# Two PSUM banks for the second part's products, and the scores' transposes in the scores' bank

## The chip, the cores and the metric

The kernel runs on one core of a Trainium2 chip. The metric is the device time of one execution in microseconds. A core has a matrix engine (PE, with its weight loads shown apart as PEld), a vector engine (DVE), an activation engine (ACT), a general engine (POOL), and a queue (SP) that here only issues transfers. PE writes its products into PSUM, which DVE and ACT read; the kernel uses PSUM as eight banks of 128 partitions by 512 fp32 columns.

## The reference

`x` and `v` have the shape (4, 11456, 128). A filter made by a small network from position embeddings is convolved with `x*v` along the sequence, the result is multiplied by `x`, and every token then goes through a top-1 mixture of 8 experts:

```python
h_filt = (np.maximum(pos_emb @ w1, 0.0) @ w2) * np.exp(-0.01 * pos)[:, None]
y = irfft(rfft(x * v, 2 * S) * rfft(h_filt, 2 * S))[:, :S]      # along the sequence
x = (x * y).reshape(B * S, D)
...
do_compute = x @ w_skip > 0
xc = x[do_compute]
logits = xc @ w_gate
e_idx = np.argmax(logits, axis=1)
gate_w = softmax(logits)[np.arange(len(xc)), e_idx]
for e in range(E):
    mask = e_idx == e
    y[mask] = gate_w[mask, None] * (np.maximum(xc[mask] @ w1[e], 0.0) @ w2[e])
out[do_compute] = xc + y
```

## The kernel before

The convolution is done as a discrete Fourier transform written as matmuls. `first_phase` and `freq_phase` do the forward transform, the product with the filter and most of the way back; they leave an intermediate array `zd` in DRAM. `out_phase`, the second part, does the last step of the transform, the multiplication by `x`, the choice of expert for every token, and the lists of tokens by expert. The experts' matmuls start inside it (`early_slots`) and go on after it (`late_slots`).

The second part goes over 32 chunks (`ch`) of 3 blocks (`blk`). All its instructions are put in order by hand: each function of a chunk or block has a lag in steps and a rank inside a step, and every engine runs its instructions in that order. In a step, by rank:

- `produced` (rank 0): `product` makes y by two matmuls (line 1031, PE; the profile shows four, as each fp32 one is done in two passes) from `zt`, loaded from `zd`, and DVE multiplies y by `x` into `xm` (line 1032). After it one piece of the experts' work is issued: matmuls into `mh` (lines 706 to 708) with their activation on ACT (`h`, line 732), copies of an expert's weights (`ws`, line 678, and `wd`, line 771), transposes of gathered tokens (line 695) with their copy (`hl`, line 697), or the second matmuls into `bank[2]` (line 789).
- `exp` (rank 1, ACT, line 1084).
- `score2` (rank 2): PE transposes the copied scores `lt` into `lgp` (line 1058) and ACT copies them to `lg` (line 1061).
- `choose` (rank 3, DVE).
- `turn` (rank 4): four transposes of the block before into `tp` (line 1044), copied by ACT to `xT` (line 1046).
- `total`, `measure`, `lay` (rank 4.4, lines 1105, 1121, 1136), `count` and `ranks` (rank 4.5, lines 1097, 1143 and 1144), `collect` (line 1176): small matmuls of the lists, once for a chunk.
- `score` (rank 4.9): four column groups of scores into `lp` (line 1052; eight in the profile), copied by ACT to `lt` (line 1054).
- `counted` (rank 6): ACT copies the counts `mine` (line 1101).

`route` reads the ranks `rk` on DVE (line 1150) ahead of `produced` in its step. The waits between engines are put in from what each instruction reads and writes; the code has no semaphores of its own.

PSUM of the second part before: one bank for `y`, one for `tp`, four called `bank` (0: the scores `lp` and the counts `mine`; 1: the small matrices of the lists; 2: the experts' second products; 3: the transposed scores `lgp`), two for `mh`.

Of the kernel before, what the change touches and what calls it, by code (L numbers as in the profile page):

```python
# [10 lines left out]
F32 = mybir.dt.float32  # L11
# [6 lines left out]
PSUM = bass.MemoryType.PSUM  # L18

B, S, D = 4, 11456, 128  # L20
E, F = 8, 1024
# [4 lines left out]
NS = NB * B  # L26
# [928 lines left out]
def out_phase(tc, i, out, zd, ex, consts):  # L955
# [6 lines left out]
    with (  # L962
        tc.tile_pool(name="slot", bufs=2, reuse_waits="tile") as eb,
    ):
      with (
        tc.manual_schedule(),
        tc.tile_pool(name="ob", bufs=2, reuse_waits="tile") as ob,
        tc.tile_pool(name="oz", bufs=2, reuse_waits="tile") as oz,
        tc.tile_pool(name="opy", bufs=1, space=PSUM, reuse_waits="tile") as opy,
        tc.tile_pool(name="opt", bufs=1, space=PSUM, reuse_waits="tile") as opt,  # L970
        tc.tile_pool(name="opl", bufs=1, space=PSUM, reuse_waits="tile") as opl,
        tc.tile_pool(name="eps", bufs=2, space=PSUM, reuse_waits="tile") as eps,
      ):
        wg, val, grid, cols, odd, rev, tri, ones = consts
        ex.space(eb)
        bank = [opl.tile([128, 512], F32, name=f"bank{k}") for k in range(4)]

        lp, lgp, mine = bank[0][:, 0:128], bank[3][:, 0:128], bank[0][0:E * NS, 128:129]
        rk, places = bank[1][:, 0:E * NS], bank[1][0:PQ, 96:96 + PL]
        sizes = bank[1][0:E, 128:134].rearrange("p (a b) -> p a b", a=3)  # L980
        lies, whole = bank[1][0:PQ, 134:135], bank[1][0:E * NS, 135:136]
# [309 lines left out]
def program(tc, i, out):  # L1291
# [5 lines left out]
    with tc.tile_pool(name="mc", bufs=1) as mc:  # L1297
        wf = mc.tile([128, 2 * E * F], F32, name="wf")
        fi = First(nc, i, x1d, x1f, mc, wf)
        spare = wf[:, fi.used:]  # L1300
        c3 = mc.tile([128, 2, 128], F32, name="c3")
        first_phase(tc, fi)
        nc.scalar.dma_start(c3, i["c3"])
        nc.scalar.dma_start(zd.rearrange("p h r w -> (p h) r w")[:, H2 * 2 * K1:], i["none"])
        later = {}

        def prepare():

            later["ex"] = Experts(tc, i, out, lists, mc, wf)
            yield  # L1310
            later["consts"] = out_consts(nc, i, mc)
            for e in range(E):
                if e % 2 == 0:
                    yield
                later["ex"].weights(e, 0)

            for e in range(E):
                if e != 1:
                    yield
                later["ex"].weights(e, 1)  # L1320
        freq_phase(tc, nc, i, fi, zd, c3, spare, prepare())
        out_phase(tc, i, out, zd, later["ex"], later["consts"])
# [55 lines left out]
```

## Time and profile before

| | |
|---|---|
| median of 3 runs | 1622.03 us (1619.08 to 1622.11) |
| profiled execution | 1621.31 us, span 1619.5 us |
| busy: PE / DVE / POOL / ACT | 95% / 74% / 68% / 49% of the span |
| second part begins / its last y starts | 735 us / 1165 us |

The span is from the first to the last instruction; the rest of the execution's time lies around it. In the views, a row of the order of time has the start in us, the duration, engine, line, operation, what is written <- what is read, the shape, and how many; in square brackets stand the idle time of the engine ahead of it and what ended it. A row of waits has who waited, for whom, the total in us, how many times, and the longest.

### The profile page before, as it was taken

The numbers are of one execution on the slowest core, as the hardware profiler recorded it, in microseconds if no ns is written. First come the engines' busy times: TensorE is split into PE (matmuls) and PEld (weight loads), VectorE is DVE, ScalarE is ACT, GpSimd is POOL, SyncE is SP. The second block draws the span as 40 slices with busy tenths as digits, with TensorE's granted clock in tenths as the row PEclk, the third lists the DMA queues.
The fourth block names the chain that finished last, engine by engine and source line by source line (L and its number), as shares of the span: only waits on it lengthen the run. The fifth ranks groups of instructions, "written<-read, shape, count | busy, mean of one in ns | idle before, by whom it ended". The sixth has DMA issues, their size and how long they took to land.

```text
span 1619.5 us, 26517 instructions
## 1 busy us (share of the span) xinstructions
PE 1537.8 (95%) x8272; PEld 960.9 (59%) x8272; DVE 1197.2 (74%) x2403; ACT 794.3 (49%) x1691; POOL 1094.7 (68%) x857
## 2 busy tenths in 40 slices
PE   7985999999999999998789999999989999999997
PEld 2552444444444444443356776666777888888997
DVE  1323877888788889995868777777767777777986
ACT  3552455444544544442345444444435555556774
POOL 1112988888888878870265729846587888777885
PEclk9996999999999999998989999999999999999999
DMA  7998999999999789968967878777521111111110
GB/s 269 334 349 317 377 377 374 357 333 331 327 343 328 262 265 313 315 209 297 312 209 241 254 230 256 245 245 238 176 67 37 46 46 46 45 37 39 37 36 21
DMA packets 200644, 361.92 MB, mean 223 GB/s; under 512 B 64842, under 2 KB 141018, under 8 KB 200462
## 3 DMA queue, kind: packets, MB, share of 16 engines
q1 hardware_dynamic: 181078, 316.98, 57.7%
q0 software_dynamic: 16704, 38.89, 8.5%
q10 hardware_dynamic: 2720, 4.34, 0.9%
q8 instruction: 67, 1.10, 0.3%
q14 instruction: 75, 0.61, 0.1%
HBM read 216.96 MB, written 145.69 MB: 224 GB/s over the span
## 4 chain that ended last, share of the span: by engine, by line
PE 81%; DVE 6%; DMA 6%; issue 4%; ACT 1%; POOL 1%; SPq 1%; ACTq 0%; DVEq 0%; POOLq 0%
PE ps L405 19%; PE xp L374 12%; PE bank L789 6%; PE ps L203 5%; PE y L1031 4%; PE my L841 4%; PE my L839 4%; PE my L840 4%; PE hp L706 4%; PE hp L708 4%; PE hp L707 4%; PE tp L1044 2%; PE mh L706 2%; PE bank L1052 1%; DMA ox<-xo 1%
## 5 line engine op out<-in xcount | busy, mean ns | idle before, releaser
L405 PE MATMUL ps<-y,c 128*128 128x512 f32 x720 | 331.3, 597 | 0.3
L472 POOL TENSOR_TENSOR y<-y,p 128x2048 f32<-128x2048 f32 x59 | 267.9, 4541 | 68.7 <-DVE p L394 68.7
L712 POOL DMA_INDIRECT out<-o,ids x186 | 202.9, 1091 | 136.9 <-DVE o L719 97.5
L405 PEld LDWEIGHTS ps<-y,c 128*128 128x128 f32 x720 | 133.4, 190 | 173.0 <-issue 155.1
L643 POOL DMA_INDIRECT xt<-out,ids x186 | 195.7, 1052 | 50.4 <-issue 32.1
L394 DVE TENSOR_TENSOR p<-xp,g 128x1024 f32<-128x1024 f32 x240 | 217.4, 947 | 0.0
L394 DVE TENSOR_TENSOR y<-xp,g 128x1536 f32<-128x1536 f32 x120 | 210.8, 1757 | 4.1
L828 DVE SCALAR_TENSOR_TENSOR hh<-hp,hh 128x1024 fp32r<-128x1024 f32 x130 | 158.4, 1218 | 66.7 <-ACT hh L827 66.7
L406 ACT COPY z<-ps 128x512 f32<-128x512 f32 x180 | 105.6, 586 | 178.2 <-PE ps L405 164.2
L827 ACT ACTIVATE hh<-hp 128x1024 fp32r<-128x1024 f32 x130 | 134.2, 1033 | 69.0 <-PE hp L708 69.0
L473 POOL TENSOR_TENSOR y<-y,p 128x1024 f32<-128x1024 f32 x59 | 139.0, 2357 | 4.6
L683 DVE TENSOR_TENSOR ws<-wf,ws 128x1024 fp32r<-128x1024 f32 x104 | 126.7, 1218 | 13.8 <-ACT ws L678 12.4
L616 POOL MEMSET idle<- 128x512 f16 x248 | 134.5, 542 | 0.3
L706 PE MATMUL hp<-hl,ws 128*128 128x512 f32 (+1 forms) x344 | 123.6, 359 | 2.2 <-DVE hh L828 1.4
L203 PE MATMUL ps<-wf,c 60*120 60x384 f32 x512 | 111.0, 530 | 13.7 <-DVE wf L186 13.6
L1031 PE MATMUL y<-zt,c 128*64 128x512 f32 x384 | 111.7, 648 | 12.7 <-DVE xm L1032 7.0
L374 PE MATMUL xp<-x,wf 128*128 128x480 f32 x256 | 117.8, 585 | 5.8 <-DMA x<-x1f 3.3
L789 PEld LDWEIGHTS bank<-wd,h 128*128 128x128 f32 x896 | 105.2, 194 | 29.6 <-issue 29.6
L205 ACT COPY wf<-ps 120x384 f32<-120x384 f32 x256 | 105.5, 493 | 28.0 <-PE ps L203 27.5
L708 PE MATMUL hp<-hl,ws 128*128 128x512 f32 (+1 forms) x344 | 116.3, 338 | 0.0
L841 PE MATMUL my<-hh,ws 128*128 128x512 f32 (+1 forms) x344 | 116.3, 338 | 0.0
L839 PE MATMUL my<-hh,ws 128*128 128x512 f32 (+1 forms) x344 | 116.2, 338 | 0.0
(165 smaller groups left out, 2996.9 us busy)
## 6 DMA issues: line engine op xcount, KB each, us to landing
wf<-xv SPq DMA_DIRECT2D x64, 768.0 KB
x1d<-wf SPq DMA_DIRECT2D x64, 720.0 KB
x<-x1d SPq DMA_DIRECT2D x60, 768.0 KB
zt<-zd SPq DMA_DIRECT2D x60, 768.0 KB
zd<-z SPq DMA_DIRECT2D x110, 384.0 KB
out<-xm SPq DMA_DIRECT2D x96, 258.0 KB
ox<-xo SPq DMA_DIRECT2D x96, 256.0 KB
x1f<-fx POOLq DMA_DIRECT2D x16, 720.0 KB
```

The lines of the kernel that those rows point to most:

```text
L203: nc.tensor.matmul(ps[p], self.c1[rows], u[rows, q * RUN:(q + 1) * RUN], start=True, stop=True)
L374: nc.tensor.matmul(xp[:, k, 0:(NS + NB) * DH], c2(n % PER * KS + j * KH + k), x1[:, j * KH + k], start=True, stop=True)
L394: nc.vector.tensor_tensor(o[:, :, :, j * KH:(j + 1) * KH].rearrange("p s a k b d -> p (s a) k b d"), x[:, None].broadcast_to([128, m, KH, ...
L405: nc.tensor.matmul(zps, c3[:, a, :], y[:, blk, a], start=(a == 0), stop=(a == 1))
L472: nc.gpsimd.tensor_tensor(y[:, 1:], y[:, 1:], p1, ALU.add)
L643: ins = nc.gpsimd.indirect_dma_start(out=xt[:, j], out_offset=None, in_=self.rows[0:have], in_offset=bass.IndirectOffsetOnAxis(ap=ids[:, j ...
L706: nc.tensor.matmul(hp, w[:, 0, c], hl[:, 0], start=True, stop=False)
L708: nc.tensor.matmul(hp, w[:, 1, c], hl[:, 0], start=False, stop=True)
L712: ins = nc.gpsimd.indirect_dma_start(out=self.rows, out_offset=bass.IndirectOffsetOnAxis(ap=ids[:, j:j + 1], axis=0), in_=o, in_offset=Non ...
L789: nc.tensor.matmul(bank[:, j * D:(j + 1) * D], h[f][:, j * 128:(j + 1) * 128], wd[s][:, f * D:(f + 1) * D], start=(f == 0), stop=(f == F / ...
L839: nc.tensor.matmul(y, w2[:, 0, c], h[:, 0], start=(f == 0), stop=False)
L841: nc.tensor.matmul(y, w2[:, 1, c], h[:, 0], start=False, stop=(f == F // 128 - 1))
```

## The change

The pool of `y` gets a second bank, so that successive products alternate between two. The tiles called `bank` become three: `lgp` moves from bank 3 to columns 256 to 383 of bank 0, which also holds `lp` (columns 0 to 127) and `mine` (column 128). The number of PSUM banks in use stays at eight. No instruction is added or taken away, and the order on each engine is the same.

```diff
-        tc.tile_pool(name="opy", bufs=1, space=PSUM, reuse_waits="tile") as opy,
+        tc.tile_pool(name="opy", bufs=2, space=PSUM, reuse_waits="tile") as opy,
...
-        bank = [opl.tile([128, 512], F32, name=f"bank{k}") for k in range(4)]
-
-        lp, lgp, mine = bank[0][:, 0:128], bank[3][:, 0:128], bank[0][0:E * NS, 128:129]
+        bank = [opl.tile([128, 512], F32, name=f"bank{k}") for k in range(3)]
+
+        lp, lgp, mine = bank[0][:, 0:128], bank[0][:, 256:384], bank[0][0:E * NS, 128:129]
```

## The prediction

> **What bounds the kernel now.** I read the summary page first (the whole and the slices), then the busy time by stage, then the waits of PE and its weight loads inside the second part, then the order of time around single steps. The busy lines and the granted clock of the page:
>
> ```profile
> span 1619.5 us, 26517 instructions
> PE 1537.8 (95%) x8272; PEld 960.9 (59%) x8272; DVE 1197.2 (74%) x2403; ACT 794.3 (49%) x1691; POOL 1094.7 (68%) x857
> PEclk9996999999999999998989999999999999999999
> ```
>
> By stage (length, then busy time of PE, PEld, DVE, ACT, POOL with counts, then granted clock, share of the DMA engines and GB/s):
>
> ```profile
> 735.00:821.00 86.00, 69.26 (x505) 30.42 (x505) 56.66 (x209) 27.84 (x92) 20.50 (x23) 0.84 0.93 313
> 821.00:1165.00 344.00, 335.92 (x2863) 232.53 (x2862) 266.46 (x944) 162.32 (x405) 224.00 (x264) 1.00 0.75 234
> 1165.00:1217.00 52.00, 47.14 (x380) 39.26 (x379) 36.94 (x140) 18.62 (x39) 35.99 (x43) 0.97 0.28 69
> 1217.00:1619.50 402.50, 390.00 (x2313) 343.51 (x2311) 307.75 (x443) 243.15 (x299) 309.52 (x332) 0.99 0.15 39
> ```
>
> The second part begins at 735 us. Its first 86 us have the DMA engines 0.93 busy and PE at 69 of 86: loads set the pace there. From 821 to 1165 PE is busy 336 of 344 us at full clock and DMA has room: there PE's own order of instructions is the clock of the kernel, and a microsecond in which PE must stand is a microsecond of the span. Behind 1217 come the experts' last tokens, 390 of 402.5 on PE, so a shift at 1165 is handed on to the end.
>
> **The change, part by part.**
>
> *Two banks for y.* Line 1031 needs y's bank free, so it waits for the multiplication of the step before (line 1032, DVE). With two banks it waits for the one two steps back. What the wait costs now (first two rows: 735 to 821; last two: 821 to 1165):
>
> ```profile
> PE y L1031 <- DVE xm L1032: 2.8, 3, 1.2
> PEld y L1031 <- DVE xm L1032: 8.0, 14, 2.4
> PE y L1031 <- DVE xm L1032: 4.3, 5, 1.0
> PEld y L1031 <- DVE xm L1032: 6.3, 7, 1.3
> ```
>
> Between 821 and 1165 it is seven waits. Five show on PE itself with 4.3 us, the other two on the weight loads alone. In a step without such a wait, y's first weight load starts 0.20 us behind the first one of the scores' matmul ahead of it; against that the seven come to 4.9 us. I take 4.9 as the gain of this stage: y is the first PE work of a step, and when it goes early all behind it goes early; the next to need line 1032 is the transposes of line 1044, behind y and the experts' matmuls, when that multiplication has ended. The bound from the other side is nothing, if the transposes wait instead. In the first 86 us the waits are at most 8.0 us on the loads, 4.7 by the measure of 0.20 us; the loads of z and x set the pace there, so I take nothing of it and keep 4.7 for the range.
>
> *The transposes' bank.* Line 1058 (PE) writes the transposed scores, line 1061 (ACT, "lg") copies them out. Today they have bank 3; then they are columns 256 to 383 of bank 0, where line 1052 writes the scores (columns 0 to 127) and line 1097 the counts (column 128). No instruction is added, removed or made longer. What is added is an order between engines that use one bank, and this trace shows that it goes by bank and not by column. Line 1136 writes column 134 of bank 1; line 1150 (DVE) reads columns 0 to 95 of it, and line 1136's own inputs were made by DVE instructions ahead of line 1150. Still the wait that ends ahead of it is that read:
>
> ```profile
> L1136 PE MATMUL bank<-step,ge x64: 182/193/205, 763.3 to 1199.2; 8*53 8x1 f32 x64
>   DVE sel L1150: 5.7, 8
> ```
>
> So I expect lines 1097 and 1052, later in a step's PE queue than line 1058, to wait until lg has read. [...] In PE's queue line 1058 is followed by the four transposes of line 1044, sometimes lines 1105 or 1136, then 1097 once in three steps, then 1052. The new wait is free when lg ends before they come up, as in this step:
>
> ```profile
> 1018.44 0.27 PE L1058 MATMUL bank<-ident,lt 128*128 128x128 f32 x1
> 1018.75 0.19 ACT L1061 COPY lg<-bank 128x36 f32<-128x36 f32 x1 [1.71 <-PE bank L1058]
> 1019.26 0.12 PEld L1097 LDWEIGHTS <-oh 128*96 128x96 f16 x1
> ```
>
> lg ends at 1018.94, PE comes at 1019.26. But ACT is one queue, and lg stands in it behind the experts' work. In half of the steps it waits for the transpose (105.3 us in 47 of 96 over the run), in the other half ACT is late:
>
> ```profile
> L1061 ACT COPY lg<-bank x96: 169/189/199, 744.9 to 1180.2; 128x36 f32<-128x36 f32 x96
>   PE bank L1058: 105.3, 47
> ```
>
> The worst kind, with the copy of an expert's weights ("ws", 1.05 us) and of its tokens ("hl") ahead of lg:
>
> ```profile
> 918.29 0.27 PE L1058 MATMUL bank<-ident,lt 128*128 128x128 f32 x1
> 918.74 1.05 ACT L678 CAST ws<-wf 128x1024 fp32r x1
> 919.11 0.12 PEld L1097 LDWEIGHTS <-oh 128*96 128x96 f16 x1
> 919.24 0.16 PEld L1052 LDWEIGHTS bank<-xT,wg 128*32 128x32 f32 x8
> 919.69 0.37 ACT L697 CAST hl<-mh 128x256 fp32r<-128x256 f32 x1
> 920.14 0.18 ACT L1061 COPY lg<-bank 128x36 f32<-128x36 f32 x1
> ```
>
> lg ends at 920.32. How soon PE starts behind another engine's end is in this step, where y waits for line 1032 (ended 1005.45, load at 1005.51, so 0.05 to 0.06 us):
>
> ```profile
> 1004.01 0.12 PEld L1097 LDWEIGHTS <-oh 128*96 128x96 f16 x1
> 1004.06 0.18 ACT L1061 COPY lg<-bank 128x36 f32<-128x36 f32 x1
> 1004.15 0.16 PEld L1052 LDWEIGHTS bank<-xT,wg 128*32 128x32 f32 x8
> 1004.77 0.68 DVE L1032 TENSOR_TENSOR xm<-y,ox 128x512 f32<-128x512 f32 x1
> 1005.51 0.20 PEld L1031 LDWEIGHTS y<-zt,c 128*64 128x64 f32 x4 [1.20 <-DVE xm L1032]
> ```
>
> So in the step at 918 line 1097 would start at 920.37 instead of 919.11, 1.26 us late, and line 1052 with it. At 1004 it is lg's end 1004.24 plus 0.05 against 1004.01: 0.28. In a step without the count, where the experts' two activations ("h", 1.29 us) hold ACT:
>
> ```profile
> 1007.52 1.29 ACT L732 ACTIVATE h<-mh 128x512 f32<-128x512 f32 x2 [2.55 <-PE mh L708]
> 1008.65 0.16 PEld L1052 LDWEIGHTS bank<-xT,wg 128*32 128x32 f32 x8
> 1008.71 0.18 ACT L1061 COPY lg<-bank 128x36 f32<-128x36 f32 x1
> ```
>
> 1008.94 against 1008.65: 0.29. I took this difference (lg's end plus 0.05, less the start of the first of lines 1097 and 1052 behind that line 1058) for every step. From 821 to 1165 it is above zero in 29 steps: 12 of the worst kind (0.86 to 1.50, together 14.5), 3 of 0.48 or 0.49 (1.5), 13 of 0.28 or 0.29 (3.6), one of 0.12. Sum 19.7 us. The first and the last of the 29 (at each, lg's row and that of the scores; the count stands 0.13 and 0.25 ahead of the scores there):
>
> ```profile
> 827.84 0.16 PEld L1052 LDWEIGHTS bank<-xT,wg 128*32 128x32 f32 x8
> 828.45 0.18 ACT L1061 COPY lg<-bank 128x36 f32<-128x36 f32 x1
> 1163.98 0.16 PEld L1052 LDWEIGHTS bank<-xT,wg 128*32 128x32 f32 x8
> 1164.74 0.18 ACT L1061 COPY lg<-bank 128x36 f32<-128x36 f32 x1
> ```
>
> Does ACT catch up when PE stands? Not in these steps: what holds lg (h, ws, hl) starts when the experts' matmuls of the same step end, so it moves with PE. Behind the waiting instruction on PE are the next y, the experts' matmuls and line 1058 of the next step; ACT's copy of the scores, line 1054, moves by the same. So I take all 19.7. Between 735 and 821 the same measure gives five steps with 6.8 us; the first and the last of them:
>
> ```profile
> 749.61 0.17 PEld L1052 LDWEIGHTS bank<-xT,wg 128*32 128x32 f32 x8 [0.22 <-issue]
> 749.72 0.19 ACT L1061 COPY lg<-bank 128x36 f32<-128x36 f32 x1 [2.02 <-PE bank L1058]
> 806.33 0.12 PEld L1097 LDWEIGHTS <-oh 128*96 128x96 f16 x1
> 807.28 0.17 ACT L1061 COPY lg<-bank 128x36 f32<-128x36 f32 x1
> ```
>
> The loads can hide it, so I take nothing and keep 6.8 for the range. In the other direction line 1058 now also waits for the reading of the counts (line 1101), which ACT does next behind line 1054's copy, which line 1058 awaits anyway, and y and the experts' matmuls lie between: nothing.
>
> *Sum.* 19.7 − 4.9 = +14.8 us. The profiled execution took 1621.3 us (span 1619.5), 0.7 below the median of the three runs, 1622.0; on the median that is 1636.8, and I say 1637. 0.2%, about what a measurement can tell from no change, is 3.2 us.
>
> **The rivals.**
>
> *No wait for other columns (faster).* If lines 1052 and 1097 need not wait for lg because the columns differ, the new bank costs nothing and y's waits are won: 4.9, at most 4.9 + 4.7 = 9.6 us, so 1612 to 1617. [...] It decides from the point where the waits on lg stay under 4.9 us. Against it stands the row of line 1136. Chance 0.06.
>
> *The stalls are absorbed.* PE stands already, between 821 and 1165, for 344 − 336 = 8 us, and for 52 − 47 = 5 us between 1165 and 1217. If those 13 us, less the 4.9 of y, come to an end earlier than PE because PE is late, up to 8 of the 19.7 vanish; with y's full 9.6 the net is about +2, so 1624. For it: some of these are waits for DVE and for gathered tokens, which do not wait for PE. Against it: they lie in other steps than the late lg. Chance 0.07 for less than +6.
>
> *The clock falls.* In 735 to 821 the granted clock is 0.84, where PE stands most; it is 1.00 in 821 to 1165, which holds y's waits of up to 1.3 us. If standing 1.3 to 1.5 us brought the clock down in the 12 worst steps, each would cost about its own length again: +14.5, so 1651. [...] Chance 0.05.
>
> **How the numbers follow.** The forecast (a loss between +6 and +24) has 0.82, the three rivals 0.06, 0.07 and 0.05. Low end: all 9.6 of y won and some 4 us absorbed, 19.7 − 13.6 = +6, so 1628. High end: nothing won of y and most of the early 6.8 paid, 19.7 + 4 = +24, so 1646. Faster 0.06 (first rival), within 0.2% 0.05 (most of the second), slower 0.89.
>
> **What would show it.** In the trace of after: the waits of line 1031 for line 1032 are gone or nearly; new waits of lines 1097 and 1052 (their weight loads) for ACT lg appear, some 30 of them after 821 and some 20 us in sum, the longest 1.3 to 1.5 us behind ws and hl; PE's busy share in that stage falls and the stage is 13 to 17 us longer; behind it, to the end, nothing changes; the clock there stays at 1.00. The prediction is wrong if no wait for lg stands ahead of those lines, or if they do but the end of the stage has not moved.

## The result: 1.0% slower, and the profile after

The changed kernel takes 1636.1 us (median of 6 runs, 1631.0 to 1638.8) against 1620.9 us before on the same occasions; the ratio is 1.0100 with a 95% interval of 1.0085 to 1.0115. The forecast was 1637 with 1628 to 1646. The profiled execution took 1635.7 us.

The page's first lines of after: PE is as busy as before (1535.5 us against 1537.8), and the span is 14.4 us longer. The trace has 64 instructions more than the 26517 before: the weight loads of line 1044 have 80 semaphore waits more ahead of them, those of line 1031 16 fewer. The counts of work on every engine are the same.

```profile
span 1633.9 us, 26581 instructions
PE 1535.5 (94%) x8272; PEld 961.5 (59%) x8272; DVE 1200.1 (73%) x2403; ACT 797.1 (49%) x1691; POOL 1094.4 (67%) x857
```

By stage, in the same columns as before:

```profile
735.00:821.00 86.00, 67.72 (x507) 31.35 (x508) 59.65 (x217) 28.69 (x94) 20.87 (x24) 0.88 0.93 313
821.00:1181.00 360.00, 338.28 (x2864) 233.05 (x2862) 268.17 (x951) 164.83 (x407) 223.82 (x264) 1.00 0.72 225
1181.00:1232.00 51.00, 46.14 (x383) 38.39 (x382) 36.40 (x134) 18.60 (x37) 35.77 (x42) 1.00 0.28 70
```

At 821 us as many of PE's instructions are done as before (507 and 505). The next 2864 take 360 us; before, 2863 took 344. From 1181 on the rest takes 452.9 us; before, from 1165 on, it took 454.5. So the whole loss, 16 us, is in the one stage that the prediction named, and 1.6 us are won behind it. The longest waits of lines 1097 and 1052 on PE there (821 to 1181; the fourth row is from 735 to 821), and below them all idle time of PE and its loads ahead of line 1031 over the run:

```profile
PE bank L1097 <- ACT lg L1061: 11.5, 12, 1.2
PE bank L1052 <- ACT lg L1061: 3.7, 9, 0.9
PE bank L1097 <- issue: 2.0, 5, 1.2
...
PE bank L1097 <- ACT lg L1061: 6.4, 4, 2.0
...
  issue: 22.6, 80
  DMA zt<-zd: 6.0, 4
  DMA c<-c: 3.9, 3
  DMA ox<-xo: 0.2, 1
```

Line 1032 no longer stands among those that y waits for, and lg (line 1061), for which no wait of lines 1097 or 1052 was listed before, leads the list. The step that the prediction showed at 918 us, in after:

```profile
925.33 0.27 PE L1058 MATMUL bank<-ident,lt 128*128 128x128 f32 x1
925.78 1.04 ACT L678 CAST ws<-wf 128x1024 fp32r x1
926.15 0.12 PEld L1097 LDWEIGHTS <-oh 128*96 128x96 f16 x1
926.73 0.36 ACT L697 CAST hl<-mh 128x256 fp32r<-128x256 f32 x1
927.18 0.18 ACT L1061 COPY lg<-bank 128x36 f32<-128x36 f32 x1
927.41 0.16 PE L1097 MATMUL bank<-ones,oh 128*96 128x1 f16 x1 [1.18 <-ACT lg L1061]
927.50 0.16 PEld L1052 LDWEIGHTS bank<-xT,wg 128*32 128x32 f32 x8 [1.23 <-issue]
```

The weights of line 1097 are loaded at 926.15, its matmul starts at 927.41, 0.05 us behind lg's end at 927.36: 1.26 us late, the figure worked out for this step. The row says 1.18, since the idle time counts from the modelled end of the work ahead. In all 28 waits of lines 1097 and 1052 behind 821 (17.6 us with the seven, 2.4 us, that the view puts down to issue) the matmul starts 0.05 us behind lg's end.

### The profile page after: what moved, and what is told of

Read it like the earlier page. It is cut to its first block, busy times and chain, and to the rows that moved or that the text cites. A ratio compares the mean times of both kernels' runs of the same rounds, so it can differ in the third digit from the quotient of the medians.

```text
span 1633.9 us, 26581 instructions
## 1 busy us (share of the span) xinstructions
PE 1535.5 (94%) x8272; PEld 961.5 (59%) x8272; DVE 1200.1 (73%) x2403; ACT 797.1 (49%) x1691; POOL 1094.4 (67%) x857
## 4 chain that ended last, share of the span: by engine, by line
PE 81%; DMA 6%; issue 5%; ACT 3%; DVE 3%; POOL 1%; ACTq 1%; SPq 1%; DVEq 0%; POOLq 0%
PE ps L405 19%; PE xp L374 12%; PE bank L789 7%; PE ps L203 5%; PE y L1031 5%; PE hp L706 4%; PE my L841 4%; PE my L839 4%; PE hp L708 4%; PE my L840 4%; PE hp L707 4%; PE mh L706 2%; PE bank L1052 2%; PE tp L1044 1%; PE mh L708 1%
## 5 line engine op out<-in xcount | busy, mean ns | idle before, releaser
L643 POOL DMA_INDIRECT xt<-out,ids x186 | 195.7, 1052 | 48.5 <-issue 31.5
```

The source lines that it names most:

```text
L643: ins = nc.gpsimd.indirect_dma_start(out=xt[:, j], out_offset=None, in_=self.rows[0:have], in_offset=bass.IndirectOffsetOnAxis(ap=ids[:, j ...
```

## The experiments

**The bank alone.** The transposes in the scores' bank, y with one bank.

```diff
-        tc.tile_pool(name="opy", bufs=2, space=PSUM, reuse_waits="tile") as opy,
+        tc.tile_pool(name="opy", bufs=1, space=PSUM, reuse_waits="tile") as opy,
```

> The transposes in the scores' bank, but y with one bank as before (seven banks in use). Theory (PE stands at lines 1097 and 1052 until ACT has read lg, and the second bank of y wins some 5 us back): 19.7 us over before, so 1641 us, range 1636 to 1646; some 30 waits for lg behind 821 us of the trace, 18 to 22 us in sum; y's waits for line 1032 are back. Rival 1 (y's second bank wins nothing): as the changed kernel, 1636. Rival 2 (y's second bank is what costs): 1621.

Measured: 1640.9 us (1634.1 to 1646.3), ratio to before 1.0134 (1.0115 to 1.0153), that is 18.6 to 24.8 us on 1621. The profiled execution was the fastest of the five (1634.1); its waits on PE behind 821:

```profile
PE bank L1097 <- ACT lg L1061: 11.2, 11, 1.4
PE bank L1052 <- ACT lg L1061: 2.8, 7, 0.8
PE bank L1097 <- issue: 2.6, 5, 1.2
...
PE y L1031 <- DVE xm L1032: 1.6, 2, 0.8
```

With the smaller rows that the view puts down to issue or to other ACT work, lines 1097 and 1052 wait 28 times, 18.1 us in sum, at the low end of what was expected. The shared bank is the whole loss, and more than the whole; by the medians y's second bank wins 4.8 us of it back (1640.9 − 1636.1). Rival 2 falls. Rival 1 falls by those 4.8 us alone, with intervals that just touch. The trace of this pair shows less: from the 26th y to the last it is 358.4 us here and 356.5 in the changed kernel, and y's waits for line 1032 came back on PE with only 1.6 us. The pair of early versions below has nearly the same difference of medians, with intervals apart.

**The reading moved ahead of the experts' work, three times.** In each step the transpose of line 1058 and the copy lg come ahead of the experts' piece, so that ACT reads before h, ws and hl. The number and kind of instructions, and every wait between the sharers of the bank, stay.

```diff
-                for lag, rank, f in (..., (3, 2, score2), ...):
+                for lag, rank, f in (..., (3, 0.2, score2), ...):
...
-            if all(rank for rank, _, _ in todo):
-                todo = sorted(todo + [(0, lambda: None, ())], key=lambda v: v[0])
+            todo = sorted(todo + [(0.5, lambda: next(work, None), ())], key=lambda v: v[0])
             for rank, f, args in todo:
                 f(*args)
-                if rank == 0:
-                    next(work, None)
```

On the changed kernel (y with two banks, the bank shared):

> The changed kernel, with score2 (line 1058 and the copy lg) ahead of the experts' piece of each step instead of behind it, so that lg stands in ACT's queue ahead of h, ws and hl. The bank is shared as in the changed kernel, and every wait is still there. Theory (what costs is how late ACT reads lg): waits of lines 1097 and 1052 for lg under 2 us in sum, and y's 4.9 us stay won: 1616 us, range 1611 to 1620. Rival 1 (sharing the bank costs by itself, met waits too): 1630 or more. Rival 2 (the wait moves: line 1058 stands for the copy lt, line 1054): 1621 to 1630, with 5 us or more of line 1058 waiting for lt.

On the kernel before (y with one bank, the transposes in their own):

> The kernel before (one bank for y, the transposes in a bank of their own) with the same move of score2 ahead of the experts' piece. A control for the move. Theory: the move alone wins nothing, 1621 us, range 1617 to 1625. Rival (the move itself wins or costs): outside of that, and then the second experiment's time is to be read against this one.

With y's one bank and the bank shared:

> One bank for y, the transposes in the scores' bank, score2 ahead of the experts' piece. Theory: with lg read early sharing costs nothing, so within 2 us of the third experiment, about 1621; the difference of the second experiment to this one is the worth of y's second bank alone, 3 to 9.6 us. Rival (sharing costs by itself): 15 us or more above the third.

| | y's banks | transposes | score2 | us, median | ratio to before (95%) |
|---|---|---|---|---|---|
| before | 1 | own bank | late | 1619.6 to 1622.1 | |
| changed | 2 | shared | late | 1636.1 | 1.0100 (1.0085 to 1.0115) |
| bank alone | 1 | shared | late | 1640.9 | 1.0134 (1.0115 to 1.0153) |
| early | 2 | shared | early | 1617.9 | 0.9981 (0.9969 to 0.9993) |
| early | 1 | own bank | early | 1621.5 | 0.9996 (0.9981 to 1.0011) |
| early | 1 | shared | early | 1622.7 | 1.0019 (0.9999 to 1.0038) |

The move by itself wins nothing (the early row with an own bank against before). With it the shared bank costs 1.2 us by the medians, and the two intervals overlap, so it is not told from nothing; without it, it costs 18.6 to 24.8. So what costs is not the shared bank by itself but how late it is read. By the medians the second bank of y is worth 4.7 us with the early reading (1622.7 − 1617.9) and 4.8 with the late one; in the traces the stretch from the 26th y to the last is 3.3 us shorter with it in the early pair (345.5 and 342.2 us) and 1.9 in the late one. The early row with two banks is faster than before by 0.07 to 0.31%, and the fastest of all by the medians; its interval overlaps that of the early row with one bank and an own bank. All three early versions came out within the times expected.

The expectation of under 2 us of waits for lg held behind 821 but not ahead of it. PE's waits in the early version with two banks, first 735 to 821, then the three longest of 821 to 1165, then the weight loads' longest there:

```profile
PE bank L1097 <- ACT lg L1061: 6.0, 4, 1.8
...
PE bank L1176 <- POOL hl L1170: 2.6, 2, 1.3
PE bank L1058 <- ACT ct L1101: 2.0, 5, 0.4
PE mh L695 <- ACT lg L1061: 1.8, 1, 1.8
...
PEld bank L1058 <- ACT lt L1054: 23.5, 27, 1.6
```

Behind 821 neither line 1097 nor line 1052 waits for lg at all. Ahead of it 6.0 us in four steps remain, which the experts' work does not cause: in all four lg stands in ACT's queue right behind the cast tf (line 1158), which itself waits 2.4 to 4.0 us for DVE. The row of line 695 names lg too, but that line does not use lg's bank; its load starts at 824.45, 0.05 us behind the end of the first activation h (line 732) at 824.40, so h is the likelier releaser. The wait that rival 2 named is there, but on the loads: line 1058's weights come 23.5 us late in sum behind lt, while y's matmuls still run. PE itself stands 2.0 us ahead of line 1058, by the view for the copy of the counts (line 1101); the early version with an own bank has the same row with 1.5 us, so little of it can be the shared bank's.

**A dose.** One more ACT copy straight ahead of each lg, in the changed kernel and in the one before.

```diff
+        da, db = (ob.tile([128, 512], F32, name=n, bufs=1) for n in ("da", "db"))
+        nc.vector.memset(da, 0.0)
...
+            nc.scalar.copy(db, da)
             nc.scalar.copy(lgs[ch][:, blk * B:(blk + 1) * B], lgp.rearrange("p (b e) -> p b e", b=B)[:, :, 0:1 + E])
```

> The changed kernel with one more ACT copy (128x512, its result is not used, estimated at 0.55 us from the 1.05 us of the 128x1024 copy wd) straight ahead of each lg. Theory: in the trace of the changed kernel 47 of the 96 lg follow the ACT instruction ahead of them without a gap; in those the copy makes lg later by its length, in the others it runs while ACT waits for line 1058. Less the time that PE has in hand in some of them, that is 16.4 us more in 37 steps behind 821 us: 1636 + 16 = 1652, range 1647 to 1658. Rival (the loss does not hang on when lg ends): 1636 to 1639.

> The kernel before with the same ACT copy ahead of each lg, a control: nothing on PE waits for lg there and ACT has time to spare. Theory: 1619.6 to 1623, as before. Rival (ACT itself, through the copies xT, lt or the activations, sets the pace): 1630 or more, and then the fifth experiment's loss is not the bank's.

Measured: the changed kernel goes to 1660.3 us (1656.1 to 1661.8), ratio to before 1.0254 (1.0217 to 1.0291); the one before stays, 1618.3, ratio 0.9995 (0.9974 to 1.0015). So ACT has the time for one copy of 0.61 us more in each step, and in the changed kernel PE pays for a later lg. The size was missed: 24 us more than the changed kernel instead of 16, above the range given. The copy is 0.61 us long, not 0.55, which makes the same sum 18.7; the rows of the dosed kernel (lines 1100, 1054 and 1064 are what were 1097, 1052 and 1061), waits behind 821:

```profile
L1063 ACT COPY db<-da x96: 600/612/632, 743.4 to 1214.9; 128x512 f32<-128x512 f32 x96
...
PE bank L1100 <- ACT lg L1064: 22.7, 17, 1.9
PE bank L1054 <- ACT lg L1064: 10.5, 12, 1.3
```

That is 33.2 us in 29 waits against 17.6 in 28 in the changed kernel, 15.6 more, so the waits grew by about what was expected and not by 24. The path between the two users of the bank says the same. From the start of line 1058's transpose to the first matmul of the scores or counts behind it, summed over the same 71 steps (those behind 821 us), it is 71.4 us in the kernel before, 91.1 in the changed one, 91.6 with the bank alone, 107.8 in the changed one with the dose, and again 71.4 in the kernel before with the dose. What the dose cost beyond its waits is taken up in the last section.

## Why the prediction was right

*Where the time is.* PE's order between 821 and 1165 was taken as the clock of the kernel, and the stage grew by 16 us (344 to 360 for the same instructions), 13 to 17 having been named. Behind it nothing was to change; in the profiled executions 1.6 us were won there. The kernel before has one stretch of 3.4 us at half clock in that part (granted 0.50 from 1193.4 to 1196.8) that the changed one lacks (1.00 from 1181 to 1232); it accounts for at most 1.7 us of them, an estimate from 3.4 us at 0.50.

*The wait goes by bank.* The row of line 1136 waiting for line 1150 (5.7 us in 8 waits) was the ground for it. After the change lines 1097 and 1052 wait for lg (28 times behind 821, 17.6 us) though they write other columns: the first rival falls by the trace, and by the bank alone, which by that rival would have cost nothing, and cost 18.6 to 24.8 us. In the code each shared bank is also one array of 128x512, so these runs do not tell an order kept by bank from one kept by declared array. The trace shows an order that is not kept by column; what the chip would do without it, no run here shows.

*The size of the wait.* 19.7 us was summed from 29 steps; the bank alone cost 18.6 to 24.8, and the step at 925 us shows the term itself at 1.26 us. Over the 71 steps the path from line 1058 to the scores or counts grew from 71.4 to 91.1 us, which is 19.7; over all 96 steps it grew by 26.4, where the prediction had 19.7 + 6.8. The 28 waits listed come to 17.6 us, as the idle time starts at the modelled end of the work ahead; it is not a smaller loss. That ACT does not catch up when PE stands is borne out by this sum: the waits were paid in full.

*y's second bank.* 4.9 us was taken, between 0 and 9.6. The medians give 4.8 and 4.7, the traces 1.9 and 3.3, so the sign is shown (by the early pair) and the size only roughly. (The prediction's sum of 4.9 comes out with 0.20 us counted from the end of the scores' weight loads, or 0.36 from the first of them, and not with 0.20 from the first.) The upper end, with the 4.7 of the first 86 us, did not show: with y's one bank and the shared bank the stretch from the first y to the 26th is 85.0 us, in the changed kernel 85.5. Nor did the 6.8 us of waits for lg expected there show in the time of the stage: five of them are listed, with 6.7 us, and at 821 PE is as far as before.

*Absorbed stalls.* Of the 8 us that might have been absorbed, none are seen: the sum of the two terms (19.7 − 4.9) is the result (15.2 by the medians) within its interval of 13.8 to 18.6. That the sum meets the median to 0.4 us is in part luck, since the second term is known no better than said above and the clock adds up to 1.7 us.

*The clock.* "The clock there stays at 1.00" was not quite right: it fell once in the profiled execution, to 0.50 for 3.4 us at 879 us. That is at most 1.7 us, an estimate from 3.4 us at half the clock. The third rival's wholesale fall did not come, though there were 28 waits of up to 1.2 us; that each of the worst steps would cost its own length again was the author's estimate, and no run shows it. With the longer waits of the dose (up to 1.9 us) the clock fell six times.

## What to carry to other kernels

Before a PSUM tile (an array of PSUM) is moved into another's bank, look up when its reader runs, not what columns it has (here lines 1097 and 1052 waited 28 times, 17.6 us, for a reading of other columns): write down for each step when the reading ends and when the next writer of that bank stands in PE's queue. If the reader stands in a queue behind unrelated work, as lg does behind ws and hl (1.04 and 0.36 us) in the step at 925 us, the sharing puts that work on the path of PE: 1.26 us there. Moving the reading ahead of that work can take the cost away: here 1.2 us by the medians were left of 18.6 to 24.8, and that is not told from nothing. The bank that the sharing gives is worth only what its new owner waited for (here some 4.7 us of 1621 by the medians).

## What the runs showed of the hardware

In the dosed kernel PE's granted clock falls to half six times between 821 and 1205, each time for one stretch of 3.4 us (the mean over these 384 us is 0.97). In the three of these that are printed here, PE was busy about half of the 3.4 us ahead. Pairs of such stretches: three of the dosed kernel, two of the changed kernel, one of the kernel before, one of the kernel before with the dose (length, busy time of PE, PEld, DVE, ACT, POOL, then the granted clock, share of the DMA engines and GB/s):

```profile
860.50:863.90 3.40, 1.69 (x20) 1.06 (x19) 1.00 (x5) 3.19 (x10) 3.03 (x5) 1.00 0.19 41
863.90:867.30 3.40, 3.40 (x14) 2.27 (x11) 2.05 (x3) 0.57 (x3) 1.84 (x2) 0.50 0.80 180
877.60:881.00 3.40, 1.57 (x13) 1.26 (x12) 2.21 (x12) 3.03 (x8) 0.27 (x1) 1.00 0.15 3
881.00:884.40 3.40, 3.33 (x18) 1.22 (x18) 1.41 (x8) 1.34 (x5) 0.00 (x0) 0.50 0.45 155
945.80:949.20 3.40, 1.76 (x15) 1.46 (x14) 0.75 (x4) 3.21 (x8) 1.71 (x2) 1.00 0.18 14
949.20:952.60 3.40, 3.33 (x16) 1.25 (x16) 0.81 (x4) 1.34 (x5) 0.00 (x0) 0.51 0.49 155
...
875.60:879.00 3.40, 2.20 (x25) 1.55 (x25) 3.02 (x16) 2.94 (x8) 0.79 (x2) 1.00 0.17 17
879.00:882.40 3.40, 3.40 (x12) 1.85 (x9) 2.18 (x6) 0.25 (x2) 0.00 (x0) 0.50 0.57 168
892.60:896.00 3.40, 2.20 (x22) 1.80 (x24) 3.12 (x12) 3.02 (x7) 2.11 (x2) 1.00 0.15 3
896.00:899.40 3.40, 3.40 (x31) 2.39 (x32) 2.40 (x6) 0.56 (x3) 0.00 (x0) 1.00 0.58 167
...
852.10:855.50 3.40, 2.28 (x31) 2.04 (x29) 3.26 (x7) 1.95 (x5) 3.07 (x5) 1.00 1.02 341
855.50:858.90 3.40, 3.40 (x29) 2.18 (x28) 3.13 (x17) 1.13 (x3) 3.06 (x5) 1.00 0.89 320
...
1107.25:1110.66 3.41, 1.67 (x21) 1.27 (x21) 2.30 (x7) 1.46 (x4) 3.08 (x4) 1.00 0.66 173
1110.66:1114.08 3.42, 3.42 (x29) 2.48 (x25) 2.38 (x7) 0.24 (x2) 0.72 (x2) 1.00 0.92 206
```

In the dosed kernel the clock fell, in these three pairs, behind 1.57 to 1.76 us of busy time in 3.4; in the changed kernel, behind 2.20, once it did (0.50 from 879.0) and once it did not (1.00 from 896.0); in the kernel before, behind 2.28, it did not. But in the last pair it stayed at 1.00 behind 1.67, so the busy time of PE in such a stretch does not decide by itself; what else does, these runs do not show. The longest single wait for lg in the dosed kernel behind 821 was 1.9 us.

Does the clock account for the rest of the dose? From the 26th y to the last, the changed kernel and then the dosed one:

```profile
823.13:1179.66 356.53, 334.81 (x2826) 230.90 (x2822) 266.15 (x940) 163.10 (x401) 221.35 (x262) 1.00 0.72 225
...
820.78:1199.56 378.78, 342.24 (x2826) 234.64 (x2822) 268.30 (x942) 199.33 (x472) 220.86 (x263) 0.97 0.69 213
```

The dosed kernel takes 22.3 us more for the same matmuls. Its PE stands 14.8 us more (36.5 against 21.7) and is busy 7.4 us more. Six half-speed stretches against one are five more; by an estimate from 3.4 us at 0.50 they cost at most 1.7 us each, 8.5 us together, which is enough for the longer busy time. The mean granted clock of the four dosed executions is 0.969 to 0.974, of the six of the changed kernel 0.974 to 0.981. That the clock is the cause of that rest was not tested by itself. In the early versions too the clock fell behind 821: twice with the shared bank (at 838 and 855 us with y's two banks, at 842 and 859 with one; the mean from 821 to 1165 is 0.99 in both), once with the own bank (at 853; the mean there is 1.00). The one at 838 was granted 0.50 from 837.6 to 841.0.
